# Seven block products for eight in the gate projection of the last two token groups, with PSUM banks chosen one by one

## The chip, the cores and the metric

The kernel runs on one core of one Trainium2 chip. Times are device microseconds (us), the median of several runs on the chip. A profile is one profiled execution; its span leaves out some 2 us that the measured time contains. Of a profile, the page is the summary, the chain is the work that ended last, followed back through what each step waited for, and a view is any other list asked of it. The engines are PE (TensorE, matrix products), DVE (VectorE), ACT (ScalarE), POOL (GpSimd) and SP (the queue for DMA transfers); PEld marks TensorE's loads of weights.

## The reference, cut to what matters

```python
q_p, k_p = phi(q), phi(k)                       # relu, times cos and sin of the position
kv  = einsum('bhsf,bhsd->bhfd', k_p, v)
x   = einsum('bhsf,bhfd->bhsd', q_p, kv) / den  # 4608 tokens x 512
g   = x @ w_gate                                # 512 x 1536
out = (g * sigmoid(g) * (x @ w_val)) @ w_out    # 1536 x 512
```

The 4608 tokens are worked in nine groups of 512, numbered 0 to 8. For each group the kernel makes x from attention tiles (four of 128 tokens), transposes it by DMA into `xT`, projects it by the gate and value weights (twelve blocks of 128 columns each), multiplies SiLU(gate) by value into `ht`, and projects `ht` by `w_out`. The tiles of a group are made while the group before is projected. A group is cut into 16 slots, twelve in the projection and four in the output, and other work, an attention tile say, is hung on a slot. From group 2 on the output projection is done by seven block products for eight (a Strassen-like scheme: sums of blocks are formed first, one product fewer is needed).

## The kernel before: what the change and the argument touch

PSUM has eight banks, and all of them are one tile, `banks`. `take` hands out one bank, or an aligned pair (0 and 1, 2 and 3, ...), by longest out of use:

```python
banks = psum.tile([P, 8, 512], FP32, name="banks")

def take(n, hold=None, fills=False, seeded=False):
    taken = {x for r in held.values() for x in r}
    free = [b for b in range(0, 8, n) if not any(b <= x < b + n for x in taken)
            and (filled[b] or not seeded)]
    b0 = min(free, key=lambda b: (..., sorted(used[b:b + n], reverse=True)))
    ...
    touch(range(b0, b0 + n))
    return banks[:, b0] if n == 1 else banks[:, b0:b0 + n]
```

An attention tile takes a pair and does not hold it. VectorE reads both banks twice (for the denominators and for x):

```python
def a_tile2(t):
    ps = take(2)
    ...                                            # 8 matmuls into ps[:, 0] and ps[:, 1]
    x_of(t, ps)

def x_den(t, ps, ys=slice(0, 4)):
    nc.vector.tensor_scalar(out=st["den", t]..., in0=ps[:, :, 0:2 * J * D1]..., ...)
def x_mul(t, ps, ys=slice(0, 4)):
    nc.vector.tensor_tensor(out=st["x", t]..., in0=ps[:, :, 0:2 * J * D1]..., in1=st["rec", t]..., op=ALU.mult)
```

Gate and value of one block of columns are eight matmuls of 512 columns:

```python
for i in which:                                    # 0: gate, 1: value
    for kc in range(KC):                           # 4
        nc.tensor.matmul(out=st["f", tg, fc, lo][i], lhsT=(wg_sb, wv_sb)[i][:, kc, fs],
                         rhs=xT[tg][:, ts, kc], start=(kc == 0), stop=(kc == KC - 1))
```

## Time and profile before

| what | value | where |
|---|---|---|
| time | 318.56 us, median of 4 | runs |
| span of the profile | 316.2 us | page |
| TensorE busy, clock | 98%, full | page, parts 1 and 2 |
| group 7, projection part | 21.75 us | chain, 250.77 to 272.52 |
| group 8, projection part | 20.72 us | chain, 281.69 to 302.41 |
| output part of each | 9.17 and 9.18 us | chain |

The "projection part" of a group is the time from its first gate matmul to its first output matmul. In group 7 it holds four attention tiles for group 8; in group 8 none. The lines are in the prediction. The profiled execution took 317.96 us, 0.6 less than the median.

### The profile page before, as it was taken

How to read it: one execution, taken by the hardware profiler on the slowest of the kernel's cores; microseconds unless marked ns; L12 is line 12 of the kernel's file. 1: busy time of each engine (PE TensorE's matmuls, PEld its weight loads, DVE VectorE, ACT ScalarE, POOL GpSimd, SP SyncE). 2: the span in 40 equal slices, each digit the busy share in tenths (PEclk: the TensorE clock that was granted, in tenths of full speed). 3: DMA queues.
4: the chain of work that ended last, by engine and by line, in shares of the span. 5: the costliest groups of instructions: out<-in, count | busy, mean ns of one | idle time of the engine just before them, and what ended most of it. 6: DMA issues, size and time to landing. Idle time of an engine off the chain costs nothing.

```text
span 316.2 us, 6614 instructions
## 1 busy us (share of the span) xinstructions
PE 309.1 (98%) x2624; PEld 182.7 (58%) x2624; DVE 220.2 (70%) x441; ACT 134.1 (42%) x245; POOL 35.5 (11%) x60
## 2 busy tenths in 40 slices
PE   8899999999999999999999999999999999999994
PEld 4596555455445485548554765477456745774473
DVE  7873777797658888597858785879578437743652
ACT  7554545753435354335433453344433133213330
POOL 6754102000201100030003000300000000000000
PEclk9999999999999999999999999999999999999999
DMA  7999999998796985979795979598951241133004
GB/s 259 220 198 197 206 205 139 226 130 110 140 225 88 175 116 135 129 80 197 148 142 75 200 149 145 72 199 134 157 77 35 58 93 23 39 69 72 2 0 133
DMA packets 74766, 41.06 MB, mean 130 GB/s; under 512 B 49904, under 2 KB 69872, under 8 KB 74736
## 3 DMA queue, kind: packets, MB, share of 16 engines
q1 hardware_dynamic: 51952, 22.55, 39.7%
q0 software_dynamic: 22192, 17.57, 37.1%
q10 hardware_dynamic: 592, 0.52, 0.5%
q8 instruction: 20, 0.33, 0.4%
q14 instruction: 10, 0.08, 0.1%
HBM read 37.75 MB, written 9.44 MB: 149 GB/s over the span
## 4 chain that ended last, share of the span: by engine, by line
PE 86%; DVE 6%; DMA 4%; ACT 2%; issue 1%; DVEq 0%; ACTq 0%
PE banks L535 57%; PE banks L649 15%; PE banks L592 6%; DMA xT<-x 4%; PE banks L305 3%; PE banks L419 2%; DVE ht L546 1%; DVE sums L623 1%; DVE x L442 1%; PE banks L465 1%; PE banks L401 1%; DVE v L259 1%; PE banks L172 1%; PE banks L345 0%; PE banks L507 0%
## 5 line engine op out<-in xcount | busy, mean ns | idle before, releaser
L541 ACT ACTIVATE sg<-banks 128x512 bf16<-128x512 f32 (+2 forms) x116 | 65.8, 568 | 118.7 <-PE banks L535 115.6
L535 PE MATMUL banks<-xT,wg_sb 128*128 128x512 bf16 (+2 forms) x464 | 111.3, 364 | 0.3 <-DMA xT<-x 0.2
L535 PE MATMUL banks<-xT,wv_sb 128*128 128x512 bf16 (+2 forms) x464 | 111.3, 364 | 0.0
L546 DVE TENSOR_TENSOR ht<-sg,banks 128x512 f16<-128x512 bf16 (+2 forms) x116 | 74.5, 648 | 52.2 <-PE banks L535 45.5
L535 PEld LDWEIGHTS <-wv_sb 128*128 128x128 bf16 x464 | 44.9, 98 | 48.7
L535 PEld LDWEIGHTS <-wg_sb 128*128 128x128 bf16 x464 | 43.0, 98 | 42.3 <-issue 0.4
L649 PEld LDWEIGHTS <-ht 128*128 128x128 f16 x336 | 32.4, 98 | 3.9
L649 PEld LDWEIGHTS <-sums 128*128 128x128 f16 x252 | 24.6, 98 | 3.6 <-issue 0.8
L259 DVE TENSOR_TENSOR v<-raw_v,tab 128x1152 bf16<-128x1152 bf16 x31 | 22.7, 751 | 0.3 <-ACT raw_v L712 0.3
L592 PE MATMUL banks<-wo_sb,ht 128*128 128x512 f16 x96 | 22.7, 379 | 0.0
L442 DVE TENSOR_TENSOR x<-banks,rec 128x512 bf16<-128x512 f32 (+1 forms) x32 | 21.6, 674 | 1.3 <-PE banks L401 0.3
L649 PE MATMUL banks<-wo_sb,ht 128*128 128x256 f16 x168 | 20.6, 273 | 0.0
L649 PE MATMUL banks<-wt_sb,sums 128*128 128x256 f16 x168 | 19.5, 273 | 0.0
L649 PE MATMUL banks<-wt_sb,ht 128*128 128x256 f16 x168 | 19.5, 273 | 0.0
L255 DVE TENSOR_TENSOR r_q<-raw_q,tab 128x1152 bf16<-128x1152 bf16 x24 | 17.6, 752 | 2.4 <-ACT raw_q L238 2.1
L238 ACT ACTIVATE raw_k<-raw_k 128x576 bf16<-128x576 bf16 (+1 forms) x25 | 17.0, 694 | 0.0
L861 POOL COPY hold<-phit 1x2 bf16<-1x2 bf16 x5 | 1.2, 234 | 130.4 <-DMA phit<-r_q 130.4
L623 DVE TENSOR_TENSOR sums<-ht 128x1024 f16<-128x1024 f16 (+1 forms) x28 | 15.5, 552 | 0.2
L238 ACT ACTIVATE raw_q<-raw_q 128x576 bf16<-128x576 bf16 x24 | 15.0, 674 | 0.0
L592 PEld LDWEIGHTS <-ht 128*128 128x128 f16 x96 | 9.1, 98 | 8.9 <-issue 0.2
L419 PEld LDWEIGHTS <-phit 128*128 128x128 bf16 (+1 forms) x240 | 10.0, 100 | 6.5 <-issue 1.3
L664 DVE TENSOR_SCALAR ob<-banks 128x512 f32<-128x512 f32 (+1 forms) x15 | 9.8, 656 | 4.4 <-PE banks L649 3.6
(98 smaller groups left out, 223.9 us busy)
## 6 DMA issues: line engine op xcount, KB each, us to landing
out_dram<-ob SPq DMA_DIRECT2D x67, 128.0 KB, 2.4
raw_k<-in_k_dram POOLq DMA_DIRECT2D x7, 576.0 KB, 9.0
raw_q<-in_q_dram POOLq DMA_DIRECT2D x6, 576.0 KB, 6.5
raw_v<-in_v_dram POOLq DMA_DIRECT2D x6, 576.0 KB, 11.7
wo_sb<-in_moe_w_out_dram POOLq DMA_DIRECT2D x3, 512.0 KB, 12.8
wg_sb<-in_moe_w_gate_dram POOLq DMA_DIRECT2D x5, 256.0 KB, 9.0
wv_sb<-in_moe_w_val_dram POOLq DMA_DIRECT2D x5, 256.0 KB, 9.3
wo_sb<-in_v_dram SPq DMA_DIRECT2D x2, 576.0 KB, 4.1
```

The lines of the kernel that those rows point to most:

```text
L238: nc.scalar.activation(out=out, in_=in_, func=AF.Relu)
L255: nc.vector.tensor_tensor(out=st[b, "q"][:, g], in0=o.unsqueeze(2).to_broadcast([P, NC, 2, D]), in1=tab, op=ALU.mult)
L259: nc.vector.tensor_tensor(out=v2s[b % 2][:, g, :, :, 0:D], in0=(first if b == 0 and g == 0 else {"v": raw_of(b, "v")})["v"][:, g].unsqueez ...
L419: nc.tensor.matmul(out=ps[ms, e, g * D1:(g + 1) * D1], lhsT=phit[b][:, e, g, c:c + n].rearrange("p c s -> p (c s)"), rhs=kv2s[b % 2][:, e, ...
L442: nc.vector.tensor_tensor(out=st["x", t].rearrange("p (y e d) -> p e y d", e=2, d=D)[:, :, ys], in0=ps[:, :, 0:2 * J * D1].rearrange("p e ...
L535: nc.tensor.matmul(out=st["f", tg, fc, lo][i], lhsT=(wg_sb, wv_sb)[i][:, kc, fs], rhs=xT[tg][:, ts, kc], start=(kc == 0), stop=(kc == KC - 1))
L541: nc.scalar.activation(out=sg[:, 0:n], in_=st["f", tg, fc, lo][0], func=AF.Silu, scale=DOWN)
L546: nc.vector.tensor_tensor(out=ht[:, fc, r:r + n], in0=st.pop(("s", tg, fc, lo))[:, 0:n], in1=ps[1], op=ALU.mult)
L592: nc.tensor.matmul(out=o_ps[t], lhsT=ht[:, fc, r:r + P], rhs=wo_sb[:, fc], start=(fc == 0), stop=(fc == FC - 1))
L623: nc.vector.tensor_tensor(out=o[:, lo:hi], in0=x[:, lo:hi], in1=y[:, lo:hi], op=op)
L649: nc.tensor.matmul(out=to[i][:, 0] if len(to) == 2 else to[0][:, i], lhsT=a[:, kc, i * P:(i + 1) * P], rhs=b[:, kc], start=first and kc == ...
L664: nc.vector.tensor_single_scalar(out=o_, in_=p_, scalar=x, op=ALU.mult)
```

## The change

The intent is to save TensorE work, the engine that bounds the kernel: the gate projection of groups 7 and 8 by seven block products for eight. Products that share a bank's partial sums need more banks in flight, so from group 7 on `take` no longer keeps pairs aligned: a pair is the two banks longest out of use, wherever they lie. The rest makes room: fp16 for x and the weights (meant to keep the precision of the sums of blocks), fewer buffers for raw k and v and one for v, sums stored over arrays that are dead by then, one copy moved from VectorE to ScalarE. Below, u counts three thirds of four blocks of columns each; a third's seven products are summed in four banks, a, b, c and e, and "product e" is a product into bank e.

```diff
+    GATE = (7, 8)
-    raw = ctx.enter_context(tc.tile_pool(name="raw", bufs=3))
+    raw = ctx.enter_context(tc.tile_pool(name="raw", bufs=2))
+    rawq = ctx.enter_context(tc.tile_pool(name="rawq", bufs=3))
 ...
     def take(n, hold=None, fills=False, seeded=False):
         taken = {x for r in held.values() for x in r}
+        if loose[0]:
+            bs = sorted(sorted((b for b in range(8) if b not in taken and (filled[b] or not seeded)),
+                               key=lambda b: used[b])[0:n])
+            ...
+            touch(bs)
+            return banks[:, bs[0]] if n == 1 else banks[:, bs[0]:bs[1] + 1:bs[1] - bs[0]]
 ...
-    wg_sb = consts.tile([P, KC, d_ff], BF16)
-    wv_sb = consts.tile([P, KC, d_ff], BF16)
+    wg_sb = consts.tile([P, KC, d_ff], FP16)
+    wv_sb = consts.tile([P, KC, d_ff], FP16)
 ...
+    def ffn_by_quarters(tg, slot_of):
+        ...
+        for u in range(3):
+            a = bank("a", fills=True)
+            product(a, u, A11, B11, True)
+            b = bank("b", seeded=True)
+            nc.scalar.copy(out=b, in_=a)
+            e = bank("e", fills=True)
+            product(e, u, W3, X3, True)
+            m7 = m7p.tile([P, 2, HT], FP32, name="m7")
+            nc.scalar.copy(out=m7, in_=e)
+            V(*((u - 1, 1, 1) if u else (u, 0, 0)))       # a value block, 4 matmuls of 512
+            product(b, u, W2, X2, False)
+            c = bank("c", seeded=True)
+            nc.vector.tensor_tensor(out=c, in0=m7, in1=b, op=ALU.add)
+            product(a, u, A12, B21, False)
+            silu(u, 1, 0, a)
+            ...
+            product(b, u, W1, X1, False)
+            nc.vector.tensor_tensor(out=m7, in0=m7, in1=b, op=ALU.add)
+            silu(u, 0, 1, m7)
+            product(c, u, A22, X4, False)
+            silu(u, 0, 0, c)
+            ...
+            product(b, u, W4, B22, False)
+            silu(u, 1, 1, b)
 ...
-        copied("dve", C21, c)
+        copied("act", C21, c)
 ...
+            elif tg - 1 in GATE:       # slots of the next group's four tiles; in group 7: 1, 2, 5, 6
+                s = SLOTS * (tg - 1) + (... else (1, 2, 5, 6))[i]
```

More of the change, by code (lines that the diff above doesn't have):

```diff
@@ L50 @@
     HD = d_model // 2
+    KH = KC // 2
+    GATE = (7, 8)
     consts = ctx.enter_context(tc.tile_pool(name="consts", bufs=1))
-    raw = ctx.enter_context(tc.tile_pool(name="raw", bufs=3))
+    raw = ctx.enter_context(tc.tile_pool(name="raw", bufs=2))
+    rawq = ctx.enter_context(tc.tile_pool(name="rawq", bufs=3))
     rel = ctx.enter_context(tc.tile_pool(name="rel", bufs=1))
@@ L59 @@
     sgp = ctx.enter_context(tc.tile_pool(name="sgp", bufs=5))
+    sg2p = ctx.enter_context(tc.tile_pool(name="sg2p", bufs=3))
+    m7p = ctx.enter_context(tc.tile_pool(name="m7p", bufs=2))
     obp = ctx.enter_context(tc.tile_pool(name="obp", bufs=2))
@@ L71 @@
     filled = [False] * 8
+    loose = [False]
     def take(n, hold=None, fills=False, seeded=False):
         taken = {x for r in held.values() for x in r}
+        if loose[0]:
+            bs = sorted(sorted((b for b in range(8) if b not in taken and (filled[b] or not seeded)),
+                               key=lambda b: used[b])[0:n])
+            assert len(bs) == n
+            if hold is not None:
+                held[hold] = bs
+            for b in bs:
+                filled[b] = fills or seeded
+            touch(bs)
+            return banks[:, bs[0]] if n == 1 else banks[:, bs[0]:bs[1] + 1:bs[1] - bs[0]]
         free = [b for b in range(0, 8, n) if not any(b <= x < b + n for x in taken)
@@ L103, in raw_of @@
         if (b, nm) not in raws:
-            raws[b, nm] = raw.tile([P, G, NC, D], BF16, name=f"raw_{nm}")
+            raws[b, nm] = (rawq if nm == "q" else raw).tile([P, G, NC, D], BF16, name=f"raw_{nm}")
         return raws[b, nm]
@@ L158 @@
     kvd = []
+    kvt = consts.tile([P, 2, 8 * J * D1], BF16, name="kvt")
     for j in range(2):
-        t = consts.tile([P, 8 * J * D1], BF16, name=f"kvd_{j}")
+        t = kvt[:, j]
         if j:
@@ L163 @@
         kvd.append(t.rearrange("p (e j w i x) -> p e j w i x", e=2, j=J, w=2, i=2))
+    xs_sb = kvt.rearrange("p a b -> p (a b)")[:, 0:2 * KC * T // 2].bitcast(FP16).rearrange(
+        "p (n t c x) -> p n t c x", n=4, t=2, c=KH)
+    ident16 = consts.tile([P, P], FP16)
+    make_identity(nc, ident16)
     zeros = consts.tile([P, P], BF16)
@@ L210 @@
     v2s = []
+    wgs_sb = consts.tile([P, 4, KH, HC, P], FP16, name="wgs_sb")
     for j in range(2):
-        t = consts.tile([P, G, NC, 2, W], BF16, name=f"v2_{j}")
+        t = (wgs_sb.rearrange("p n c u x -> p (n c u x)")[:, 0:G * NC * 2 * W].bitcast(BF16).rearrange(
+            "p (g c e w) -> p g c e w", g=G, c=NC, e=2) if j else
+            consts.tile([P, G, NC, 2, W], BF16, name=f"v2_{j}"))
         nc.vector.tensor_copy(out=t[:, :, :, :, D], in_=csk.unsqueeze(1).to_broadcast([P, G, NC, 2]))
         v2s.append(t)
-    wg_sb = consts.tile([P, KC, d_ff], BF16)
-    wv_sb = consts.tile([P, KC, d_ff], BF16)
+    wg_sb = consts.tile([P, KC, d_ff], FP16)
+    wv_sb = consts.tile([P, KC, d_ff], FP16)
     wg_r = moe_w_gate.rearrange("(c p) f -> p c f", p=P)
@@ L259, in vmul @@
         nc.vector.tensor_tensor(
-            out=v2s[b % 2][:, g, :, :, 0:D],
+            out=v2s[b == 1][:, g, :, :, 0:D],
             in0=(first if b == 0 and g == 0 else {"v": raw_of(b, "v")})["v"][:, g].unsqueeze(2).to_broadcast([P, NC, 2, D]),
@@ L307, in kv_mm @@
                         lhsT=raws[b, "k"][es, g, c],
-                        rhs=v2s[b % 2][es, g, c, :, 0:D1],
+                        rhs=v2s[b == 1][es, g, c, :, 0:D1],
                         start=(c == 0), stop=(c == NC - 1),
@@ L359, in kv_first_out @@
             give_back(("kvf", j))
-    qf = consts.tile([P, 2, J, 2, D], BF16)
+    qf = wgs_sb.rearrange("p n c u x -> p (n c u x)")[:, G * NC * 2 * W:G * NC * 2 * W + 4 * J * D].bitcast(
+        BF16).rearrange("p (c j i d) -> p c j i d", c=2, j=J, i=2)
     qr = [lodge(4 * J * SH, BF16).rearrange("p (e j c s) -> p e j c s", e=2, j=J, c=2) for i in range(2)]
@@ L436, in x_rec @@
             st["rec", t] = smp.tile([P, H, 1], FP32, name="rec")
-            st["x", t] = xp.tile([P, d_model], BF16, name="x")
+            st["x", t] = xp.tile([P, d_model], FP16, name="x")
         nc.vector.reciprocal(out=st["rec", t].rearrange("p (e y) o -> p e y o", e=2)[:, :, ys],
@@ L487, in x_norm @@
         nc.vector.reciprocal(out=rec, in_=den)
-        x = xp.tile([P, d_model], BF16, name="x")
+        x = xp.tile([P, d_model], FP16, name="x")
         for j in range(J):
@@ L500, in xT_of @@
         if tg not in xT:
-            xT[tg] = xtp.tile([P, GH // 2, KC, P], BF16, name="xT")
+            xT[tg] = xtp.tile([P, GH // 2, KC, P], FP16, name="xT")
         return xT[tg][:, off]
     def x_turn_pe(t, ks=slice(0, KC)):
-        ps = take(1, ("xt", t, ks.start)).bitcast(BF16).rearrange("p (k x) -> p k x", x=P)
+        ps = take(1, ("xt", t, ks.start)).bitcast(FP16).rearrange("p (k x) -> p k x", x=P)
         for kc in range(ks.start, ks.stop):
-            nc.tensor.transpose(out=ps[:, kc], in_=st["x", t][:, kc * P:(kc + 1) * P], identity=ident)
+            nc.tensor.transpose(out=ps[:, kc], in_=st["x", t][:, kc * P:(kc + 1) * P], identity=ident16)
         st["xt", t, ks.start] = ps[:, ks]
@@ L558, in ffn_fc, with gate_weight_sum @@
         ffn_act(*a)
+    wg4 = wg_sb.rearrange("p (k c) (u w x) -> p w k c u x", k=2, w=2, x=P)
+    A11, A12, A21, A22 = wg4[:, 1, 0], wg4[:, 1, 1], wg4[:, 0, 0], wg4[:, 0, 1]
+    W1, W2, W3, W4 = (wgs_sb[:, i] for i in range(4))
+    X1, X2, X3, X4 = (xs_sb[:, i] for i in range(4))
+    def gate_weight_sum(n):
+        o, x, y, op = ((W1, A21, A22, ALU.add), (W2, W1, A11, ALU.subtract), (W3, A11, A21, ALU.subtract),
+                       (W4, A12, W2, ALU.subtract))[n]
+        nc.vector.tensor_tensor(out=o, in0=x, in1=y, op=op)
@@ new lines, in x_parts, with x_sum, bank, free @@
+    def x_parts(tg):
+        return (xT[tg][:, 2 * j:2 * j + 2, KH * k:KH * k + KH] for k in range(2) for j in range(2))
+    def x_sum(tg, n):
+        B11, B12, B21, B22 = x_parts(tg)
+        o, x, y = ((X1, B12, B11), (X2, B22, X1), (X3, B22, B12), (X4, B21, X2))[n]
+        nc.vector.tensor_tensor(out=o, in0=x, in1=y, op=ALU.subtract)
+    def ffn_by_quarters(tg, slot_of):
+        B11, B12, B21, B22 = x_parts(tg)
+        val, gates, count = {}, {}, [0]
+        def bank(nm, **kw):
+            return take(1, ("g", tg, nm), **kw).rearrange("p (i x) -> p i x", i=2)
+        def free(nm):
+            give_back(("g", tg, nm))
+        def product(to, u, a, x, first):
+            for i in range(2):
+                for c in range(KH):
+                    nc.tensor.matmul(out=to[:, i], lhsT=a[:, c, 2 * u + i], rhs=x[:, :, c],
+                                     start=first and i == 0 and c == 0, stop=c == KH - 1, skip_group_check=True)
+        def silu(u, w, j, src):
+            if (u, w) not in gates:
+                gates[u, w] = sg2p.tile([P, 2, T], BF16, name="sg2")
+            nc.scalar.activation(out=gates[u, w][:, :, j * HT:(j + 1) * HT], in_=src, func=AF.Silu, scale=DOWN)
+        def V(u, i, w):
+            fc = 4 * u + 2 * i + w
+            val[u, i, w] = take(1, ("v", tg, fc), fills=True)
+            for kc in range(KC):
+                nc.tensor.matmul(out=val[u, i, w], lhsT=wv_sb[:, kc, fc * P:(fc + 1) * P], rhs=xT[tg][:, :, kc],
+                                 start=(kc == 0), stop=(kc == KC - 1))
+        def mul(u, i, w):
+            fc = 4 * u + 2 * i + w
+            nc.vector.tensor_tensor(out=ht[:, fc], in0=gates[u, w][:, i], in1=val.pop((u, i, w)), op=ALU.mult)
+            give_back(("v", tg, fc))
+        def done():
+            slot_of(count[0])
+            count[0] += 1
+        for u in range(3):
[7 more added lines that the diff above has]
+            nc.scalar.copy(out=m7, in_=e)
+            free("e")
+            V(*((u - 1, 1, 1) if u else (u, 0, 0)))
+            done()
+            product(b, u, W2, X2, False)
[3 more added lines that the diff above has]
+            silu(u, 1, 0, a)
+            free("a")
+            if u:
+                mul(u - 1, 1, 1)
+            V(u, 0, 0) if u else V(u, 1, 0)
+            done()
+            product(b, u, W1, X1, False)
[3 more added lines that the diff above has]
+            silu(u, 0, 0, c)
+            free("c")
+            V(u, 1, 0) if u else V(u, 0, 1)
+            done()
+            if u == 2:
+                for n in (1, 2):
+                    token_sum(n, 0, 4)
+            mul(u, 0, 0)
+            mul(u, 1, 0)
+            if u == 2:
+                token_sum(3, 4, 6)
+            product(b, u, W4, B22, False)
+            silu(u, 1, 1, b)
+            free("b")
+            if u:
+                V(u, 0, 1)
+            mul(u, 0, 1)
+            if u:
+                done()
+                token_sum(*((3, 0, 4) if u == 1 else (4, 0, 4)))
+        V(2, 1, 1)
+        mul(2, 1, 1)
+        for n in (1, 2):
+            token_sum(n, 4, 6)
+        done()
@@ L895 @@
         at(tk[-1] + 1, lambda b=b: kv_free(b))
+    for n in range(4):
+        at(SLOTS * (1 + n * (GATE[0] - 1) // 4) + FC + 3, lambda n=n: gate_weight_sum(n))
+    for tg in GATE:
+        for n in range(4):
+            at(SLOTS * (tg - 1) + FC + (2, 2, 3, 3)[n], lambda tg=tg, n=(2, 0, 1, 3)[n]: x_sum(tg, n))
     for t in range(2 * OUT, NTG * OUT):
@@ L908 @@
                 s = SLOTS * 2 + t - 4
+            elif tg - 1 in GATE:
+                s = SLOTS * (tg - 1) + ((1, 2, 7, 9) if tg < 6 else (1, 2, 4, 7) if tg < 8 else (1, 2, 5, 6))[i]
             at(s, lambda t=t: a_tile2(t), turn(t))
@@ L911 @@
         s0 = SLOTS * tg
-        for fc in range(FC):
+        if tg in GATE:
+            loose[0] = True
+            ffn_by_quarters(tg, lambda i: slot(s0 + i))
+        for fc in range(FC) if tg not in GATE else ():
             ffn_fc(tg, fc)
```

## The prediction

> **What bounds the kernel now.** I read three views, in this order: the page, for the engine that never rests; the chain of waits, for how that engine divides its time in the last two token groups; and VectorE's instructions in order of time, for how close together it can issue, since the change gives it new work.
>
> The page:
>
> ```profile
> PE 309.1 (98%) x2624; PEld 182.7 (58%) x2624; DVE 220.2 (70%) x441; ACT 134.1 (42%) x245; POOL 35.5 (11%) x60
> ...
> PEclk9999999999999999999999999999999999999999
> ...
> L541 ACT ACTIVATE sg<-banks 128x512 bf16<-128x512 f32 (+2 forms) x116 | 65.8, 568 | 118.7 <-PE banks L535 115.6
> L535 PE MATMUL banks<-xT,wg_sb 128*128 128x512 bf16 (+2 forms) x464 | 111.3, 364 | 0.3 <-DMA xT<-x 0.2
> L535 PE MATMUL banks<-xT,wv_sb 128*128 128x512 bf16 (+2 forms) x464 | 111.3, 364 | 0.0
> L546 DVE TENSOR_TENSOR ht<-sg,banks 128x512 f16<-128x512 bf16 (+2 forms) x116 | 74.5, 648 | 52.2 <-PE banks L535 45.5
> ```
>
> TensorE is busy 98% at full clock, and the gate and value projections (L535) waited 0.3 us in the whole run. The other engines wait for TensorE: the SiLU on ScalarE sat idle 115.6 us before it got a gate, the product on VectorE 45.5 us. So a microsecond of TensorE work removed is a microsecond of the end, as long as no new wait takes its place.
>
> The chain of waits, last two groups:
>
> ```profile
> 250.77 10.36 PE banks L535 x48
> 261.13 0.26 PE banks L419 x8
> 261.38 3.45 PE banks L535 x16
> ...
> 272.52 9.17 PE banks L649 x84
> 281.69 20.72 PE banks L535 x96
> 302.41 9.18 PE banks L649 x84
> ```
>
> Columns are start, length, what. A 512-column matmul takes 20.72 / 96 = 215.8 ns, and a 256-column one in the output projection, which already uses the seven-product scheme (L649, 84 matmuls for one group), takes 9.17 / 84 = 109.2 ns. The reported means (364 and 273 ns) include a pipeline tail and are not what a matmul costs in a stream. Group 7 (250.77 to 281.69) holds four attention tiles of 0.26 us (L419) for group 8; group 8 holds none.
>
> VectorE in order of time (start, duration, instruction), a busy stretch of group 6:
>
> ```profile
> 239.14 0.69 DVE L442 TENSOR_TENSOR x<-banks,rec 128x512 bf16<-128x512 f32 x1
> 239.75 0.68 DVE L546 TENSOR_TENSOR ht<-sg,banks 128x512 f16<-128x512 bf16 x1
> 240.34 0.68 DVE L623 TENSOR_TENSOR sums<-ht,sums 128x1024 f16<-128x1024 f16 x1
> 240.95 0.42 DVE L623 TENSOR_TENSOR sums<-ht 128x512 f16<-128x512 f16 x1
> 241.28 0.68 DVE L546 TENSOR_TENSOR ht<-sg,banks 128x512 f16<-128x512 bf16 x1
> ```
>
> Starts are 0.60 us apart for the large forms and 0.33 us for the small one, though durations read 0.68 and 0.42. I count a queue by the first pair, and a wait for one result by the second.
>
> **What the Trainium skill says.** "TensorE: Matmul & The Clock Gate", section "Back-to-back issue gap", gives N / 2.4 + 2.5 ns for an isolated warm gap: 215.8 ns for 512 columns and 109.2 for 256, exactly this trace. The same section says a real stream of 512-column matmuls goes at about 131 ns; the trace says 215.8 and decides. "Perfetto Trace Analysis", section "Optimizing Scalar/DVE Operations", says that profiled latency contains a write acknowledgement that overlaps the next instruction; 0.60 against 0.68 us agrees. "PSUM — Partial Sum Buffer", section "PSUM bank collisions raise a hardware error", wants any two engines kept apart on a bank: so TensorE cannot add to a bank while VectorE or ScalarE reads it. No row of the kernel before prices that; the new scheme does it in six places per third of a group.
>
> **The change, part by part.**
> Gate products. Per group the gate now takes 12 x 4 = 48 matmuls of 512 columns: 48 x 215.8 = 10.36 us. After: three thirds, each of seven products of four 256-column matmuls, so 84 x 109.2 = 9.17 us. Saved 1.19 us per group, 2.37 us for two. The value projection keeps its 10.36 us. The PE-only length of the projection part goes from 20.72 to 19.53 us in group 8, and from 21.75 to 20.56 in group 7.
>
> ScalarE. Two bank copies per third (bank to bank, and to m7) at 0.57 us: 6 x 0.57 = 3.4 us per group, beside 7.2 us of SiLU. About 10.6 of 20 us, so no bound. Also the copy of C21 leaves VectorE for ScalarE in seven groups: 0.6 us each, off the path on both.
>
> VectorE. Two additions per third on 512 fp32 values (as L546, 0.60 apart): 3.6 us per group. Four token sums of xT, 512 fp16 each, 0.33: 1.3 us, placed in the preceding output projection, which has room (4.9 us busy of 9.5 in group 6). Four weight sums of 1536 fp16 values, about 0.95 us as the L614 rows have it, once, at the ends of groups 1, 2, 4 and 5.
>
> Older groups. FP16 for BF16 leaves all sizes the same, and the fp16 output matmuls already run at the pace that the formula gives. Two buffers for raw k and v instead of three, and one v buffer from batch 2 on: each load or product that overwrites one comes at least eight slots behind its last reader (product of batch b-1 at slot 5 of its group, overwrite at slot 15 or later), so no wait. The second identity costs GpSimd 0.19 + 0.29 us before a copy that waited 1.8 us for a load. All this: 0, give or take 0.2 us.
>
> Group 7, walked by hand. VectorE's queue in the projection part: 12 products 7.2, additions 3.6, four attention tiles at 0.20 + 0.24 + 0.61 = 1.05 each 4.2, output token sums 4 x 0.60 + 3 x 0.33 = 3.4: 18.4 of 20.6 us, 89%. That is too full for waits inside it to vanish. With t = 0 at the group's start and 0.2 us from a matmul's slot to its reader (as 250.60 to 250.80 at the group's start):
> - Tile 33's matmuls end at 5.73. VectorE reads them from 5.95 to 7.08, since tile 32 and an addition went ahead. Banks of attention tiles are not held until read; by longest out of use, the second third's product e falls on one of tile 33's two banks and wants it at 6.61. Wait 0.5 us.
> - Tiles 34 and 35 and three products queue from 12.4; the value matmuls of column 7 meet a bank that product 6 lets go late: 0.15 us. The addition into c of the last third comes at 16.9 to 17.6, while TensorE wants to add to that same bank b at 17.36: 0.25 us.
> - At the end, the last product and two sums must precede the third output product: 24.6 against 24.57, some 0.1 us.
> Sum 1.0 us, against 1.19 saved there. Group 8 has no tiles: its queue is 14.2 of 19.5 us, the same walk puts every read ahead of its bank's next write (the last sums at 22.45 against 22.64). I keep the whole 1.19 us.
> Total: 1.19 + (1.19 - 1.0) = 1.4 us, rounded up to 1.5 as the hand walk takes each wait at its worst. 318.6 - 1.5 = 317.1 us.
>
> **The rivals.**
> 1. No new wait counts: 2.4 us, 316.2 us. For it: the seven-product output projection runs 84 matmuls at 109.2 ns with no gap, and value matmuls (0.86 us each) stand between most hand-overs. Against: VectorE at 89% in group 7.
> 2. VectorE becomes the bound in group 7 and ScalarE's longer chain (copy, copy, four SiLUs) adds waits in both groups: waits of 2.5 us or more in total, a wash or slightly slower, 318.6 to 319.5. For it: two engines now sit inside each product chain where none did. Against: group 8's VectorE has a quarter of its time free.
> 3. The weight sums delay earlier groups. At the ends of groups 3 and 4 the chain runs over VectorE and then 6.8 us of a transpose into xT that lands when TensorE needs it, so 0.5 us there would be 0.5 us of the end. Against: the sums' ends are groups 1, 2, 4 and 5, half a group before such a tile, with idle gaps of 0.4 to 1.0 us per slot on VectorE between.
>
> **Range and chances.** The largest conceivable gain is 2.4 us, 0.75% of 318.6; so faster by 2% (312.2) is out of reach, and slower by 2% (325.0) needs over 8 us of new waits in two groups of 30 us each. 316.2 to 318.2 holds rival 1 at its edge and most of a part of rival 2, with 0.2 us of scatter. Faster 0.01, within 2% 0.98, slower 0.01.
>
> **What would show it.** Right: 84 gate matmuls per group 109 ns apart; the stretch from the start of group 8's projections to the start of its output 1.2 us shorter than 20.72; group 7's from start to output between 21.2 and 22, with waits of TensorE for VectorE at the second and last third, around tile 33's bank and the addition into c; nothing moved before group 7. Wrong: group 7 with no waits (then 316.2), group 8 with waits above 0.3 us for ScalarE or VectorE, matmuls above 115 ns apart, or TensorE waiting for xT at an earlier group's start.

## The result, and the profile after

The changed kernel takes 320.31 us (320.13 to 320.33, four runs) against 318.56 us before. The ratio is 1.0054, 95% interval 1.0037 to 1.0072. The prediction was 317.1 us, and the time lies above its range: the change made the kernel slower, not faster, though by half a per cent only.

The page of the changed kernel, the line that answers to the first one shown of before (L560 is now the gate and value of groups 0 to 6, L617 a gate product, L629 a value block, L782 the output):

```profile
PE 306.7 (96%) x2696; PEld 189.6 (60%) x2696; DVE 228.6 (72%) x458; ACT 143.6 (45%) x264; POOL 35.8 (11%) x62
```

TensorE's busy time did fall, by 2.4 us, and the span rose by 2.3 us. So TensorE now waits. For what, the view of waits says, restricted to TensorE (who waited, for whom, us in total, times, longest):

```profile
PE banks L617 <- DVE x L467: 3.6, 3, 1.5
```

Three waits, all for VectorE's multiplication that reads an attention tile. The first and the third in order of time (the bracket is the idle time before the instruction and what ended it; the second, 1.53 us, is shown with e1 below):

```profile
258.27 0.60 PE L617 MATMUL banks<-xT,wg_sb 128*128 128x256 f16 x4 [0.86 <-DVE x L467]
...
268.78 0.60 PE L617 MATMUL banks<-kvt,wgs_sb 128*128 128x256 f16 x4 [1.20 <-DVE x L467]
```

The chain of waits of the changed kernel in group 7, the view of which the prediction shows groups 7 and 8 of before (start, length, what):

```profile
251.25 0.87 PE banks L617 x8
...
256.72 0.27 PE banks L444 x8
...
257.52 0.70 DVE x L467
...
258.27 1.03 PE banks L617 x8
...
264.69 0.70 DVE x L467
...
265.43 0.60 PE banks L617 x4
...
268.04 0.70 DVE x L467
...
268.78 0.60 PE banks L617 x4
...
275.88 9.31 PE banks L782 x84
285.19 0.87 PE banks L617 x8
...
304.72 9.33 PE banks L782 x84
```

Read it as a list of starts. Group 7's projection part goes from 251.25 to 275.88: 24.63 us, where 20.56 was the length without a wait and about 21.6 was predicted. Group 8's goes from 285.19 to 304.72: 19.53 us, to the hundredth what was predicted. At 258.27, 265.43 and 268.78 TensorE goes on only when an `x L467` has ended.

The difference of the spans, part by part: group 7 +2.88 (24.63 - 21.75), group 8 -1.19, the two outputs +0.14 and +0.15, a later start of group 7 (251.25 against 250.77) +0.48, a shorter tail -0.16: together +2.30 = 318.5 - 316.2. The later start is chance: e2, e3, e7 and e8, whose programs are the same up to there, start group 7 at 250.47 to 250.97. (The spans differ by more than the medians, because the profiled execution of before was a fast one.)

Why should a gate product wait for an attention tile? The built program answers, if each matmul's semaphore wait is traced to the instruction that releases it, and the banks of both are written down:

```text
TensorE, second third, product a -> bank 5    waits for VectorE's read of tile 33, banks 4 and 6
TensorE, second third, product b -> bank 3    waits for VectorE's read of tile 34, banks 0 and 4
TensorE, last third,   product e -> bank 4    waits for VectorE's read of tile 35, banks 1 and 6
VectorE's first read of tile 34, banks 0 and 4    waits for ScalarE's SiLU of c, bank 1
```

In none of the four do the two instructions share a bank. In all of them the bank waited for lies between the two banks of the pair. That is theory A: in the built program an instruction on two banks that are not neighbours is guarded as if it touched every bank from the first to the last. Theory B is the prediction's second rival: VectorE is full in group 7, and TensorE waits for its queue wherever the banks lie.

### The profile page after: what moved, and what is told of

Same layout as the page of the kernel before. It is cut to its first block, busy times and chain, and to the rows that moved or that the text cites. A ratio compares the mean times of both kernels' runs of the same rounds, so it can differ in the third digit from the quotient of the medians.

```text
span 318.5 us, 6778 instructions
## 1 busy us (share of the span) xinstructions
PE 306.7 (96%) x2696; PEld 189.6 (60%) x2696; DVE 228.6 (72%) x458; ACT 143.6 (45%) x264; POOL 35.8 (11%) x62
## 4 chain that ended last, share of the span: by engine, by line
PE 88%; DVE 4%; DMA 4%; ACT 1%; issue 0%; SPq 0%; DVEq 0%; ACTq 0%
PE banks L560 45%; PE banks L782 18%; PE banks L725 6%; PE banks L629 6%; PE banks L617 6%; PE banks L329 3%; DMA xT<-x 2%; PE banks L444 2%; DMA wo_sb<-in_v_dram 2%; DVE x L467 1%; PE banks L490 1%; PE banks L426 1%; DVE ht L571 1%; DVE sums L756 1%; PE banks L193 1%
## 5 line engine op out<-in xcount | busy, mean ns | idle before, releaser
L560 PE MATMUL banks<-xT,wg_sb 128*128 128x512 f16 (+2 forms) x368 | 86.6, 360 | 0.1
L560 PE MATMUL banks<-xT,wv_sb 128*128 128x512 f16 (+2 forms) x368 | 86.6, 360 | 0.0
L566 ACT ACTIVATE sg<-banks 128x512 bf16<-128x512 f32 (+2 forms) x92 | 51.5, 560 | 76.2 <-PE banks L560 74.1
L571 DVE TENSOR_TENSOR ht<-sg,banks 128x512 f16<-128x512 bf16 (+2 forms) x92 | 58.0, 638 | 29.8 <-PE banks L560 22.7
L560 PEld LDWEIGHTS <-wv_sb 128*128 128x128 f16 x368 | 35.5, 98 | 37.4
L560 PEld LDWEIGHTS <-wg_sb 128*128 128x128 f16 x368 | 33.9, 98 | 31.7 <-issue 0.4
L782 PEld LDWEIGHTS <-ht 128*128 128x128 f16 x336 | 32.5, 98 | 4.2
L782 PEld LDWEIGHTS <-sums 128*128 128x128 f16 x252 | 24.5, 98 | 4.1 <-issue 0.8
L629 PE MATMUL banks<-xT,wv_sb 128*128 128x512 f16 x96 | 24.3, 379 | 0.0
L467 DVE TENSOR_TENSOR x<-banks,rec 128x512 f16<-128x512 f32 (+1 forms) x32 | 21.6, 675 | 1.3 <-PE banks L426 0.3
L782 PE MATMUL banks<-wo_sb,ht 128*128 128x256 f16 x168 | 20.6, 273 | 0.0
L782 PE MATMUL banks<-wt_sb,sums 128*128 128x256 f16 x168 | 19.8, 273 | 0.0
L782 PE MATMUL banks<-wt_sb,ht 128*128 128x256 f16 x168 | 19.5, 273 | 0.0
L634 DVE TENSOR_TENSOR ht<-sg,banks 128x512 f16<-128x512 bf16 x24 | 15.6, 681 | 2.9 <-ACT sg L623 2.4
```

The lines of the kernel that those rows point to most:

```text
L467: nc.vector.tensor_tensor(out=st["x", t].rearrange("p (y e d) -> p e y d", e=2, d=D)[:, :, ys], in0=ps[:, :, 0:2 * J * D1].rearrange("p e ...
L566: nc.scalar.activation(out=sg[:, 0:n], in_=st["f", tg, fc, lo][0], func=AF.Silu, scale=DOWN)
L571: nc.vector.tensor_tensor(out=ht[:, fc, r:r + n], in0=st.pop(("s", tg, fc, lo))[:, 0:n], in1=ps[1], op=ALU.mult)
L629: nc.tensor.matmul(out=val[u, i, w], lhsT=wv_sb[:, kc, fc * P:(fc + 1) * P], rhs=xT[tg][:, :, kc], start=(kc == 0), stop=(kc == KC - 1))
L782: nc.tensor.matmul(out=to[i][:, 0] if len(to) == 2 else to[0][:, i], lhsT=a[:, kc, i * P:(i + 1) * P], rhs=b[:, kc], start=first and kc == ...
```

## The experiments

Twelve runs followed, of ten more kernels, with the changed kernel and e9 each run once more at the end. The seventh to tenth looked for a better version, too. Times are compared through the kernel before, which ran in the same rounds. All outputs are right.

| run | time, us | before in its rounds | ratio (95%) | group 7's projection part, us |
|---|---|---|---|---|
| changed kernel | 320.31 | 318.56 | 1.0054 (1.0037 to 1.0072) | 24.63 |
| e1_split | 316.80 | 318.10 | 0.9961 (0.9940 to 0.9981) | 21.44 |
| e2_adjacent | 316.80 | 318.10 | 0.9958 (0.9935 to 0.9982) | 21.59 |
| e3_adjheld | 317.62 | 318.10 | 0.9986 (0.9969 to 1.0003) | 22.63 |
| e4_rest | 317.76 | 318.10 | 0.9988 (0.9972 to 1.0005) | 21.75 |
| e5_wide_old | 328.90 | 318.56 | 1.0323 (1.0284 to 1.0363) | 32.57 |
| e6_gate8 | 316.62 | 318.56 | 0.9940 (0.9917 to 0.9963) | 21.75 |
| e7_retouch | 317.16 | 318.56 | 0.9956 (0.9928 to 0.9984) | 22.05 |
| e8_retouch8 | 317.43 | 318.56 | 0.9966 (0.9942 to 0.9990) | 21.96 |
| e9_early | 315.76 | 318.60 | 0.9907 (0.9888 to 0.9927) | 19.53 |
| e10_early2 | 319.31 | 318.60 | 1.0018 (0.9999 to 1.0037) | 19.53 |
| e11_again (changed kernel) | 319.75 | 318.64 | 1.0031 (1.0015 to 1.0048) | 24.62 |
| e12_early_again (as e9) | 315.72 | 318.64 | 0.9902 (0.9885 to 0.9919) | as e9 |

### e1_split: the same banks, read one bank at a time

```diff
-        x_den(t, ps); x_rec(t, ps); x_mul(t, ps)
+        for e in range(2):                       # group 7 only
+            nc.vector.tensor_scalar(out=den[:, 4 * e:4 * e + 4], in0=<bank e of the pair>, ...)
+        nc.vector.reciprocal(out=rec, in_=den)
+        for e in range(2):
+            nc.vector.tensor_tensor(out=<half e of x>, in0=<bank e of the pair>, in1=rec[:, 4 * e:4 * e + 4], ...)
```

> Same banks as the changed kernel, but in group 7 each attention tile's two banks are read by separate VectorE instructions (one per bank), so no instruction spans the banks between them. Theory A (a pair two or four banks apart is treated as the whole range from first to last bank, so TensorE's next product on a bank in between waits for the read of the tile): the second wait (1.53 us in the changed kernel) and the third (1.20 us) go, the first (0.86 us) shrinks to about 0.5 us because product e really does take a bank of tile 33; the extra VectorE work is 0.25 us per tile. The projection part of group 7 goes from 24.6 us to about 21.5 us, the time from 320.3 to about 317.5 us. Theory B (VectorE is simply full in group 7 and TensorE waits for its queue): with 1 us more VectorE work the waits grow, projection part 25 us or more, time 320.3 to 321.

Measured: 316.80 us. The stretch of group 7 in this run (columns: stretch, us, then busy time and instructions of PE, PEld, DVE, ACT, POOL, then the granted clock of TensorE, the share of DMA and GB/s):

```profile
250.56:272.00 21.44, 21.08 (x166) 13.98 (x165) 18.25 (x43) 9.86 (x18) 0.00 (x0) 1.00 0.35 75
```

The same stretch of the changed kernel:

```profile
251.25:275.88 24.63, 21.04 (x166) 14.01 (x165) 17.78 (x35) 10.01 (x18) 0.00 (x0) 1.00 0.30 66
```

VectorE does more work in group 7 (43 instructions for 35, 18.25 us busy for 17.78), on the same banks, and the part is 3.2 us shorter. Theory B falls with that. (Reads of one bank also let that bank go sooner. That this is not the cause is shown by e2 and e5, which keep the old reads and change the banks.) The reader should also see how the false guard reached VectorE. In the changed kernel the read of tile 34 began only at 264.25 although the tile's matmuls were issued at 263.48, because it waited for a SiLU:

```profile
263.48 0.42 PE L444 MATMUL banks<-kv,phit 128*128 128x65 bf16 x8
263.63 0.58 ACT L623 ACTIVATE sg<-banks 128x512 bf16<-128x512 f32 x1
264.25 0.17 DVE L454 TENSOR_SCALAR den<-banks 128x8 f32<-128x8 f32 x1 [1.18 <-ACT sg L623]
...
264.69 0.69 DVE L467 TENSOR_TENSOR x<-banks,rec 128x512 f16<-128x512 f32 x1
265.43 0.60 PE L617 MATMUL banks<-xT,wgs_sb 128*128 128x256 f16 x4 [1.53 <-DVE x L467]
```

ScalarE reads bank 1, VectorE wants banks 0 and 4, TensorE wants bank 3: three engines in one row, with no bank in common. At tile 33 the first read began 0.53 us after the row of the matmuls (256.55 to 257.08); by that the read of tile 34 would have begun at 264.01, so this false wait is an estimated 0.24 us of the 1.53.

### e2_adjacent: a pair is two neighbours again, at any start

```diff
-            bs = sorted(sorted((b for b in range(8) if ...), key=lambda b: used[b])[0:n])
+            ok = [b for b in range(8) if ...]
+            runs = [list(range(b, b + n)) for b in ok if all(x in ok for x in range(b, b + n))]
+            bs = min(runs, key=lambda r: sorted((used[x] for x in r), reverse=True))
```

> A pair is again two neighbouring banks (any start, not only an even one), all else as in the changed kernel. Theory A: no bank lies between, so the waits of 1.53 and 1.20 us go; the third-starting product e still lands on a bank of tile 33, a real wait of about 0.5 us. Projection part of group 7 about 21.3 us, time about 317.2 us. Theory B: 320 us, waits unchanged in sum.

Measured: 316.80 us, part 21.59 us. With no bank in between, one wait for a tile's read is left in the view of waits:

```profile
PE banks L618 <- DVE x L468: 0.4, 1, 0.4
```

This one is real: product e of the second third is given a bank of tile 33, as the prediction had walked it. Together, 21.59 - 20.56 = 1.03 us are lost in group 7, against a predicted sum of 1.0: 0.58 us at product e, 0.15 at tile 35, 0.06 at a value block and 0.25 before the addition into c of the last third. The numbers are the start of each group of matmuls in the trace less the start at the full pace.

### e3_adjheld: neighbours, held until the next slot

```diff
-        ps = take(2)
+        ps = take(2, ("at", t) if loose[0] else None)
 ...
     def slot(s):
+        for h in [h for h in held if h[0] == "at"]:
+            give_back(h)
```

> Neighbouring banks, and a tile's two banks stay held until the next slot, so that they count as used later and go out again later. Theory A with the real reuse of tile 33's bank as the rest: all waits for the tiles' reads go, what is left is VectorE's addition against TensorE on the same bank, 0.3 us or less. Projection part of group 7 20.6 to 21.0 us, time 0.4 us below the neighbouring-banks run, about 316.8 us. If the order of banks were not what matters, it equals the neighbouring-banks run.

A miss: 317.62 us, part 22.63 us, one microsecond longer than with neighbours alone. TensorE's waits in this run:

```profile
PE banks L618 <- ACT sg L624: 0.5, 1, 0.5
PE banks L630 <- DVE ht L635: 0.5, 1, 0.5
PE banks L618 <- DVE ht L635: 0.4, 1, 0.4
```

The wait for the tile is gone, and three others have come: for a SiLU on ScalarE and for VectorE's products, which still read the banks that now come out first. Holding two banks for a tile leaves six for the products, and by the built program the three waits are real: in each, the reader has the same bank (3, 2 and 4).

### e4_rest: everything but the gate products and the loose banks

```diff
-    GATE = (7, 8)
+    GATE = ()
-    for n in range(4):
-        at(SLOTS * (1 + n * (GATE[0] - 1) // 4) + FC + 3, lambda n=n: gate_weight_sum(n))
```

> Everything of the change except the gate by seven products and the loose choice of banks: fp16 for x and the weights, one more identity, two buffers for raw k and v, one v buffer, the copy of C21 on ScalarE. Prediction's claim: within 0.2 us of before, 318.6 us. Rival: the 0.5 to 0.8 us by which the changed kernel's groups 3 to 7 started later in its profile is a cost of these parts; then 319.1 us or more and the first projection starts 0.5 us later or more in this profile also.

Measured: 317.76 us against 318.10, ratio 0.9988 with 1 inside the interval. The fp16 types, the smaller pools and the moved copy cost nothing. Its group 7 starts at 250.45 us, before's at 250.77, so the later start in the first profile of the changed kernel does not come from these parts.

### e5_wide_old: the old gate, pairs as far apart as they go

```diff
 # on top of e4_rest, with loose[0] = True in groups 7 and 8
-            bs = sorted(sorted((b for b in range(8) if ...), key=lambda b: used[b])[0:n])
+            ok = [b for b in range(8) if ...]
+            bs = [min(ok), max(ok)] if n == 2 else [min(ok, key=lambda b: used[b])]
```

> The old eight-product gate (the kernel of the rest-of-the-change run), but in groups 7 and 8 a pair is taken as far apart as the free banks allow (0 and 7 for all four tiles). Theory A (a far pair is waited for as the whole range): TensorE's next gate product after each of the four tiles waits for VectorE to have read the tile. In the kernel before, the first tile ended at 261.22 us and was read by 262.96, so about 1.5 us of wait for each tile, 5 to 7 us in all: projection part of group 7 27 to 29 us instead of 21.75, time 323 to 325 us, although VectorE has the work of before. Theory B (a crowded VectorE makes the waits, the distance of the banks does not): no change, 317.8 us.

Measured: 328.90 us, more than expected. VectorE has the work of before; what has changed is the choice of banks, above all the distance within a pair. In the built program the first product after each tile goes to bank 3, 6, 5 and 3, and waits for the read of banks 0 and 7. The rows of TensorE after each of the four tiles:

```profile
263.08 1.02 PE L560 MATMUL banks<-xT,wg_sb 128*128 128x512 f16 x4 [1.63 <-DVE x L467]
...
269.18 1.02 PE L560 MATMUL banks<-xT,wg_sb 128*128 128x512 f16 x4 [2.23 <-DVE x L467]
...
275.28 1.80 PE L560 MATMUL banks<-xT,wg_sb 128*128 128x512 f16 x4 [2.23 <-DVE x L467]
...
283.41 1.49 PE L782 MATMUL banks<-wo_sb,ht 128*128 128x256 f16 x12 [2.55 <-DVE x L467]
```

The four waits are 8.64 us. Against e4_rest the projection part of group 7 lost 32.57 - 21.75 = 10.82 us. The profile calls the 0.16 us after a matmul's slot busy too (the pipeline's tail: 0.379 us reported against 0.216 us apart), which adds 4 x 0.16 = 0.64 us. The rest is the clock. The row at 275.28 takes 1.80 us for what took 1.02, and the granted clock of that stretch (the first number behind the busy times) fell:

```profile
261.09:275.28 14.19, 8.11 (x57) 4.01 (x55) 8.14 (x17) 2.39 (x4) 0.00 (x0) 1.00 0.09 18
275.28:278.60 3.32, 3.32 (x9) 1.19 (x10) 0.00 (x0) 0.60 (x1) 0.00 (x0) 0.52 0.20 40
```

At 0.52 of the clock for 3.32 us, some 3.32 x 0.48 = 1.6 us are lost. 8.64 + 0.64 + 1.6 = 10.9 us, the 10.82 but for rounding. The cut in the clock did not come each time: of the four timed runs one had a mean clock of 1.000 and a span of 325.6 us, where the profiled one has 0.994 and 327.2. So theory A was right in mechanism here, the size was larger than expected, and a second cost came on top.

### e6_gate8: seven products in group 8 alone

```diff
-    GATE = (7, 8)
+    GATE = (8,)
```

> The seven products in group 8 alone, where no attention tile asks for a pair. Group 8's projection part 19.53 us as in the changed kernel, group 7's 21.75 us as before, output of group 8 0.14 us longer. Against the rest-of-the-change run 1.19 - 0.14 = 1.05 us less: about 316.7 us.

Measured: 316.62 us, and the two projection parts:

```profile
250.61:272.36 21.75, 21.75 (x130) 10.47 (x129) 14.59 (x28) 7.17 (x12) 0.00 (x0) 1.00 0.29 64
281.53:301.06 19.53, 19.53 (x134) 12.92 (x133) 13.81 (x23) 9.77 (x18) 0.00 (x0) 1.00 0.23 55
```

Half of the change, where no pair is taken, gives its 1.19 us in full. TensorE has no idle time in either stretch (busy equals length).

### e7_retouch and e8_retouch8: a better order of banks, a later tile

```diff
 # e7, on top of e2: at the next slot a tile's banks count as used anew
+        if loose[0]:
+            late.append((now[0], [x for x in range(8) if used[x] == now[0]]))
     def slot(s):
+        while late:
+            stamp, bs = late.pop()
+            touch([b for b in bs if used[b] == stamp])
 # e8, on top of e7
-                s = SLOTS * (tg - 1) + (... else (1, 2, 5, 6))[i]
+                s = SLOTS * (tg - 1) + (... else (1, 2, 5, 8))[i]
```

> Neighbouring banks as in the second run, and a tile's banks are put at the end of the order again at the next slot, without being held in between. Product e of the second third no longer gets a bank of tile 33; the value product behind it does, 0.44 us later. Of the four waits left with neighbouring banks (0.58, 0.15, 0.06, 0.25) the first shrinks to 0.15 us: projection part of group 7 about 21.1 us, time 0.4 us below the neighbouring-banks run, 316.4 us.

> As the run before, with the last attention tile moved from slot 6 to slot 8 of group 7, so that VectorE's addition into c of the last third does not queue behind it. The 0.25 us wait goes, the 0.15 us at tile 35 too; a sum at the end may come 0.1 to 0.3 us later. Projection part of group 7 20.7 to 20.9 us, time about 316.1 us.

Both miss. e7 takes 317.16 us, against before the same as e2 (ratio 0.9956 for 0.9958), with a part of 22.05 us (250.56 to 272.61), longer than e2's. As in e3 the wait for the tile goes and two of 0.5 us come, for a SiLU and for a product on VectorE:

```profile
257.25 0.60 PE L621 MATMUL banks<-xT,wg_sb 128*128 128x256 f16 x4 [0.53 <-ACT sg L627]
265.36 0.60 PE L621 MATMUL banks<-kvt,wgs_sb 128*128 128x256 f16 x4 [0.49 <-DVE ht L638]
```

In e8 the first of these waits stays (0.53 us), the second shrinks, the 0.25 us before the addition into c, which the later tile was to take away, stay, and a wait of 0.32 us for a token sum comes in the output; with a part of about 21.96 us its time of 317.43 us is no better. The expectation had followed one wait to its bank and not asked who still reads the bank that is handed out in its place.

### e9_early and e10_early2: no tiles in group 7

```diff
-                s = SLOTS * (tg - 1) + ((1, 2, 7, 9) if tg < 6 else (1, 2, 4, 7) if tg < 8 else (1, 2, 5, 6))[i]
+                s = SLOTS * (tg - 2) + (8, 10, 12, 14)[i]        # e10: (6, 8, 10, 12)
```

> The changed kernel with group 8's four attention tiles asked for in group 6 (slots 8, 10, 12 and 14) instead of group 7 (slots 1, 2, 5 and 6), where pairs are still taken the old way. Group 7 then holds no tile, as group 8 does: projection part of group 7 19.53 us, so both groups keep their 1.19 us. Group 6 gets 4 x 0.26 us of matmuls and 4.2 us of VectorE, which had 17.2 of 23.0 us busy there. If group 6 takes it without a wait: 317.8 (the rest of the change) - 2.4 + 0.3 (two outputs 0.14 longer) = 315.7 us. If the waits only move to group 6: 317 us or more.

> As the run before, with the tiles at slots 6, 8, 10 and 12 of group 6, between the slots of group 7's own tiles, so three of them fall in the projection part, where VectorE has less room than in the output part. If VectorE's room in group 6 does not matter, the same 315.7 us; if it does, slower than the run before by some tenths of a microsecond, with the wait in group 6's second half.

e9 takes 315.76 us, as expected, and beats both kernels. Its stretches, group 6's projection, group 6's output, group 7's and group 8's projection:

```profile
218.23:241.90 23.67, 23.67 (x226) 11.87 (x224) 19.10 (x37) 9.90 (x18) 0.00 (x0) 1.00 0.64 114
241.90:251.69 9.79, 9.79 (x102) 8.81 (x103) 7.92 (x21) 2.36 (x4) 0.00 (x0) 1.00 0.26 52
251.69:271.22 19.53, 19.53 (x135) 12.89 (x133) 13.81 (x23) 9.76 (x18) 0.00 (x0) 1.00 0.27 62
280.53:300.05 19.52, 19.52 (x134) 12.88 (x133) 13.80 (x23) 9.75 (x18) 0.00 (x0) 1.00 0.23 55
```

In all four, TensorE is busy from end to end. The tiles' own work has moved, and nothing waits for it.

e10 is slower (319.31 us), as expected in direction, but for another reason than the one expected. The chain of waits shows what its first tile waited for:

```profile
226.40 8.46 DMA phit<-r_q
...
234.91 0.30 PE banks L444 x4
```

At slot 6 the transposed queries of the last batch have not landed; TensorE waits 2.7 us for them. VectorE has no part in it. Slot 8 in e9 is late enough.

### e11_again and e12_early_again

> The changed kernel once more. In its first profile the second half of the first load of v came late and every group from 1 on started 0.5 to 0.8 us later than before, which none of the other runs with the same start showed. If that is chance, this profile starts group 3 at 120.3 to 120.7 us and the projection part of group 7 still takes 24.6 us; time 319.9 to 320.3 us. If it belongs to the kernel, group 3 starts at 121.1 again.

> The kernel with the four tiles in group 6 on the same chip and in the same rounds as the changed kernel: 315.8 us, 4.4 us below it (3 x 1.35 of waits and the rest of its 4.1 us over the wait-free length, give or take 0.4).

The changed kernel again: 319.75 us, group 3 at 120.54 us (121.12 in its first profile, 120.32 before), group 7's projection part 24.62 us. So the 24.6 us belong to the kernel, and the late start of group 3 does not. Group 7 begins late here as well, at 251.51, for another reason: a wait of 1.0 us for a transfer into `xT` at an earlier group's start (0.3 us or less in the other profiles). The version with early tiles in the same rounds: 315.72 us, 4.03 us less, where 4.4 give or take 0.4 was expected.

## Why the prediction was wrong

The step that failed is the prediction's walk through group 7: "VectorE reads them from 5.95 to 7.08 [...] the second third's product e falls on one of tile 33's two banks and wants it at 6.61. Wait 0.5 us.", and the sum of 1.0 us that it opens. The walk let a tile's read hold up only what wants one of the tile's own two banks. What the runs showed in its place: a read of two banks that are not neighbours holds up every bank between them, too. That replaced the sum of 1.0 us by 4.07 us (24.63 - 20.56): three idle times of 0.86, 1.53 and 1.20 us, which are 3.59, and 3 x 0.16 us of pipeline tail that the profile calls busy. The line of the diff that does it was read: a pair became `banks[:, bs[0]:bs[1] + 1:bs[1] - bs[0]]`. It was taken for a choice of banks, not for a new kind of access. (Part of the first wait would have come anyway, 0.44 us later at product e: that is the 0.5 us of the walk, and e2 shows it.) The prediction's second rival came near in size by luck: VectorE was not the bound.

Point by point:

- **TensorE bounds the kernel, a matmul of 256 columns costs 109.2 ns, of 512 215.8.** Right. Group 8's projection part is 19.53 us as predicted, and TensorE's busy time fell by 2.4 us.
- **The older groups, the fp16 types, the buffers: 0 give or take 0.2 us.** Right as far as it can be told: e4_rest is 0.34 us below before, and its interval contains 1. The weight sums of the gate are not in e4_rest; e3, which has them, starts group 7 at 250.47 us and e4_rest at 250.45, so rival 3 falls too.
- **Group 7 loses 1.0 us.** Wrong in the changed kernel, for the reason above. Where pairs are neighbours (e2) the loss is 1.03 us; its first three terms differ a little (0.58 at product e for 0.5; 0.15 and 0.06 for 0.15), the addition into c is 0.25 as walked. (The 0.1 at the end belongs to the output part, so 0.9 us of the sum stand against the 1.03.) With the very banks of the changed kernel, read one by one (e1), the loss is 0.88 us. So the working was near for the program it had in mind, though the agreement to 0.03 us is luck, and the program was another. (It also counted six places per third where TensorE adds to a bank that another engine has touched; the code has five.)
- **Group 8 keeps its whole 1.19 us.** Right in the projection; each output after a seven-product gate is 0.14 us longer (9.31 and 9.33 for 9.17 and 9.18), where 0.1 was put down for group 7 and nothing for group 8. In e2 a load of weights in group 8's output was idle 0.24 us for the last token sum. That this is all of the 0.14 us is not shown.
- **Rival 1, no new wait.** Right where no tile is read: group 8, and in e9 both groups, have 19.53 us and no idle time.
- **Rival 2, VectorE as the bound.** Its time (318.6 to 319.5) was nearer to the measurement, and the stated range left it out; but its reason falls: with more work on VectorE and the same banks (e1), the kernel is 1.30 us below before where the changed one is 1.75 us above it.
- **The sum.** -2.37 for the products, +4.07 in group 7, +0.29 in the outputs: +2.0 us. Measured +1.75 us in the medians, and +1.1 in the second set of runs.

What stays open: whether the chip would have borne the accesses without these waits. The waits are put into the program when it is built. No kernel here takes a wait away while the access stays; e1 and e2 change the access. Open too is why e9 and e12 lie 2.84 and 2.92 us below before, where -2.37, +0.29 and e4_rest's -0.34 make 2.42.

## What to carry to other kernels

When an allocation changes, look at the shape of the accesses that it hands out, not only at which buffers: in these programs two neighbouring PSUM banks in one instruction held up no third bank (before, e2), and two that lay apart held up the next use of a bank between them (1.6 to 2.6 us each time in e5). Trace each new wait in the built program to the instruction that releases it, and ask whether the two share anything; here three waits of TensorE for reads of other banks, one of them lengthened by a fourth such wait on VectorE, made 3.6 us. And where a faster stage has no room for what other stages have put into it (the tiles in group 7), move that out before you tune the order of buffers: moving it brought the kernel 2.84 us below before, the best order of banks (e2) 1.30 us, and finer orders of banks gave nothing more.

## What the Trainium skill lacked or had wrong

- No page has it: the built program guards an access to two PSUM banks apart over the banks between, too. In the changed kernel TensorE sat idle 0.86, 1.53 and 1.20 us for reads of banks that it did not want, and 8.64 us in all with pairs of banks 0 and 7 (e5).
- "TensorE: Matmul & The Clock Gate", section "Back-to-back issue gap": about 131 ns for each 512-column matmul in a real stream. The profiles here have 215.8 ns in streams of 48 to 96 matmuls; the page's formula for the isolated gap (N / 2.4 + 2.5 ns) holds in the stream as well, at 256 columns too (109.2 ns).
- The same page, section "HAM oscillation — how this bites in real kernels", gives as the rule that TensorE must have no idle gap above about 3.4 us. In e5 gaps of 1.63, 2.23 and 2.23 us, with some 3.9 us of matmuls between each two of them, were followed by a granted clock of 0.52 for 3.3 us in the profiled run, so gaps below 3.4 us can cost clock too; one of four runs kept 1.000. (The page's section "A second HAM failure mode: psum-queue depth-cycling" tells of micro-idle times that swing the clock, but gives them no length.)
- "PSUM — Partial Sum Buffer", section "Summary: rules for kernel authors", says that a seed written by VectorE or ScalarE for an accumulation must be 0. The seven-product gate starts two accumulations per third from a partial sum that ScalarE or VectorE wrote, in banks that a full-width matmul had filled earlier, and all its runs were correct. The page's longer rule (such a matmul adds where an earlier one has left its mark) agrees; the summary's rule is stricter than these runs needed.
